# A chunked state-space scan fused with a feed-forward layer: operands at one SBUF offset, weight sums made once, another spread of the second-layer groups, later loads

## The chip, the core and the metric

The kernel runs on one core of a Trainium2 chip. Its engines are TensorE (PE in the profile; its weight loads, PEld, overlap its matmuls), VectorE (DVE), ScalarE (ACT), GpSimd (POOL) and SyncE (SP), which issues all DMAs here. The metric is the device time of the whole program in microseconds, the median of three runs.

## What is computed

The reference, cut to what matters (4 batches, 8 heads, 768 steps, head size 32, state size 16; 3072 tokens, model width 256, hidden width 2048; float32 data):

```python
# per chunk of the sequence, with state carried from chunk to chunk
cum = np.cumsum(log_a_chunk, axis=-1)
L = np.exp(cum[..., :, None] - cum[..., None, :]) * causal
M = np.einsum('bhin,bhjn->bhij', Cc, Bc) * L
y = np.einsum('bhij,bhjd->bhid', M, xc) \
    + np.einsum('bhin,bhnd->bhid', Cc, state) * np.exp(cum)[..., None]
state = np.exp(sum_log_a) * state + sum_j(Bc * xc * np.exp(cum[-1] - cum))
# y, reordered to tokens x (heads*head size) = 3072 x 256, goes through
h = y @ w_in                      # 256 -> 2048; the weights come as float64
g = np.maximum(0.01 * h, h)
return (g @ w_out).astype(np.float32)
```

## The kernel before

**Numbers.** Every float32 product is made of three TensorE matmuls on rounded halves: weight high by data high, weight low by data high, weight high by data low (`wh`, `wl`; `xh`, `xl`; `gh`, `gl`). A "product" of a 128x128 weight block with a 128x512 tile is so three matmuls of 512 columns, called large matmuls below. The weights arrive as the bits of float64 numbers (`raw`, 16 blocks `f` of 512 KB); DVE turns each into a float32 tile by five passes (abs L365, hold L372, shift L378, sign L385, low L392), ACT rounds it to `wh` (L404), POOL subtracts to `wl` (L405). `PASSES` says how many passes stand in each step.

**Startup.** Decay sums and masks are made, partly by a round trip through DRAM (`parts` to `left_d` and `right_d`, back as `dl` and `dr`), and the first three chunks of 48 steps are scanned (`LEAD`). `fetch_w` loads a weight block, `fetch_c` a chunk's B and C (`bcn`), `fetch_x` its inputs (`xs`); all are issued by SP in the order of the code, and an issue that must wait for a buffer holds what comes behind it. `keep_warm` issues matmuls on the zero tile `idle`.

**Plain phase.** 32 steps, each for one of the first two token tiles (512 tokens) and one weight block: `ffn_in` (L434, six large matmuls), `ffn_out` three steps later (L458, six). Every second step also carries the work of one of the chunks 3 to 15 (scores L283, chunk products L308 and L316, states L334 and L341, decay L250), and all carry decoding passes.

**Last phase.** `two_tiles` works on two pairs of token tiles, eight blocks `p` for each pair. In a block a pair of weight blocks meets a pair of tiles by seven products instead of eight (L627): A(a11), B(s2), C(s1), A(a12), B(s3), B(a22), C(s4). The `s` are sums of weight blocks (`weight_sums`, POOL, L575 and L584; split into halves by ACT L589 and POOL L590), made in the block before and again for the second pair. The data operands are sums of tiles, made by `combine` (L601 to L618): for the first pair at the end of the plain phase, for the second in the first pair's blocks. A is a PSUM tile of its own; B and C are the two halves of one PSUM tile, and a product that writes one of them waits until DVE has read what it must of the tile: after s2 and s1 `u2` (L696), after s3 `u3` and `c22` (L703, L704), after a22 and s4 `c21` and `c12` (L710, L711). ACT and DVE then make `gh` and `gl` (L663, L664; L667). Four second-layer groups of a block (`two_out`, L652, six large matmuls each) go into `queue`, and `slot()` issues the next one at fixed places of the block: one after C(s1), one after B(s3), two at the end. The queue starts with the last three `ffn_out` of the plain phase. A block has 21 + 24 = 45 large matmuls.

**Order.** The instructions of an engine stand in the order of the code. Tiles have places in SBUF given by pools; the byte offset that matters for the change is a tile's address modulo 2048: 1152 for `wh`, `wl`, `gh`, `gl` and the plain tiles, 2016 for the weight sums and the tiles of pool `qr`.

## Time and profile before

| | |
|---|---|
| median of 3 runs | 353.19 us (351.37 to 353.98) |
| profiled execution | 353.4 us, its span 351.7 us |
| granted TensorE clock, mean | 0.961 of full speed |
| busy: PE, DVE, ACT, POOL | 321.2, 239.7, 179.7, 176.2 us |
| large matmuls of the last phase | 738 from 161.16 us on |

A span is the time from the first to the last instruction that the profiler recorded; the profiled execution's own time is 1.7 us longer. All terms of the prediction are set against 353.4 us.

### The profile page before, as it was taken

To read this page: it belongs to the slowest core of one execution; us is meant where nothing else is said; L and a number is where in the kernel's file an instruction comes from. 1 tells how busy PE (TensorE), PEld (TensorE's weight loads), DVE (VectorE), ACT (ScalarE), POOL (GpSimd) and SP (SyncE) were. 2 spreads that over 40 slices of the span, in tenths; PEclk is the share of its full clock that TensorE was granted. 3 is DMA by queue.
4 is the path that set the end of the run, shared out by engine and by line. 5 is a ranking of instruction groups with operands and counts; after the bars stand their busy time and mean duration, and the time that the engine had idled before them with its cause. 6 is when DMAs were issued, how large, how long until landed. Compare 5 with 4: busy or idle time off the path is not lost.

```text
span 351.7 us, 8830 instructions
## 1 busy us (share of the span) xinstructions
PE 321.2 (91%) x3670; PEld 245.7 (70%) x3670; DVE 239.7 (68%) x359; ACT 179.7 (51%) x336; POOL 176.2 (50%) x259
## 2 busy tenths in 40 slices
PE   8737779989999998999887989999999999999994
PEld 3425657767777776888665767777776877778773
DVE  5839798999992232597868867877557575566651
ACT  4324555656666553443633554556545565455551
POOL 5406654766867335190627654675334653446100
PEclk9955889999999999999989999999999999999999
DMA  6564345363442200100010000000003000000003
GB/s 224 104 241 157 106 179 191 130 239 123 141 134 67 69 3 4 62 0 0 0 60 2 0 0 2 1 0 3 0 0 119 2 0 0 0 2 1 1 2 119
DMA packets 12224, 21.83 MB, mean 62 GB/s; under 512 B 4804, under 2 KB 5016, under 8 KB 12184
## 3 DMA queue, kind: packets, MB, share of 16 engines
q1 hardware_dynamic: 12184, 21.27, 18.3%
q8 instruction: 29, 0.48, 0.5%
q14 instruction: 11, 0.09, 0.1%
HBM read 17.82 MB, written 3.44 MB: 60 GB/s over the span
## 4 chain that ended last, share of the span: by engine, by line
PE 71%; DVE 16%; DMA 4%; issue 4%; ACT 3%; SPq 1%; POOL 0%; DVEq 0%; ACTq 0%
PE sc L627 17%; PE op L458 12%; PE sc L652 11%; PE hp L434 10%; PE op L652 7%; PE hp L627 5%; DVE u L703 3%; DVE c L704 3%; PE sc L283 2%; PE sc L316 2%; PE sc L308 2%; DMA bcn<-c_l 1%; DVE gl L667 1%; DMA left_d<-parts 1%; DMA xs<-x_l 1%
## 5 line engine op out<-in xcount | busy, mean ns | idle before, releaser
L590 POOL TENSOR_TENSOR sl<-s,sh 128x512 fp32r<-128x512 f32 x16 | 20.8, 1297 | 89.4 <-ACT sh L589 89.4
L341 POOL COPY xs<-stage 16x128 f32<-16x128 f32 x108 | 37.2, 345 | 40.5 <-ACT stage L334 35.3
L667 DVE TENSOR_TENSOR gl<-c,gh 128x512 fp32r<-128x512 f32 x48 | 48.8, 1020 | 8.8 <-PE op L652 5.9
L663 ACT ACTIVATE gh<-c 128x512 fp32r<-128x512 f32 x48 | 30.4, 633 | 43.0 <-DVE c L704 20.8
L441 ACT ACTIVATE gh<-hp 128x512 fp32r<-128x512 f32 x32 | 19.1, 598 | 41.3 <-PE hp L434 38.3
L447 DVE TENSOR_TENSOR gl<-hp,gh 128x512 fp32r<-128x512 f32 x32 | 21.9, 684 | 16.9 <-ACT hp L444 16.8
L627 PE MATMUL sc<-xh,sh 128*128 128x512 f32 x64 | 26.1, 408 | 5.6 <-DVE u L696 5.5
L664 ACT ACTIVATE c<-c 128x512 f32<-128x512 f32 x48 | 30.4, 633 | 1.5
L663 ACT ACTIVATE gh<-hp 128x512 fp32r<-128x512 f32 x16 | 9.6, 599 | 41.5 <-PE hp L627 41.5
L703 DVE TENSOR_TENSOR u<-sc,kept 128x512 f32<-128x512 f32 x16 | 11.1, 692 | 27.2 <-PE sc L627 27.2
L458 PE MATMUL op<-gh,wh 128*128 128x512 f32 x64 | 28.2, 440 | 0.6 <-DVE ob L472 0.6
L292 DVE TENSOR_TENSOR lt<-sc,lt 128x384 f32<-128x384 f32 x32 | 16.3, 550 | 17.3 <-PE sc L283 17.1
L575 POOL TENSOR_TENSOR w<-wh,wl 128x512 f32<-128x512 f32 x16 | 27.5, 1717 | 0.1
L434 PE MATMUL hp<-xh,wh 128*128 128x512 f32 x64 | 26.3, 411 | 1.2 <-ACT lt L259 0.9
L405 POOL TENSOR_TENSOR wl<-w,wh 128x512 fp32r<-128x512 f32 x16 | 22.2, 1390 | 9.0 <-ACT wh L404 8.1
L652 PE MATMUL sc<-gh,wh 128*128 128x512 f32 x64 | 25.3, 396 | 1.2 <-ACT ob L638 0.7
L434 PE MATMUL hp<-xh,wl 128*128 128x512 f32 x64 | 25.9, 405 | 0.0
L458 PE MATMUL op<-gl,wh 128*128 128x512 f32 x64 | 25.6, 400 | 0.0
L458 PE MATMUL op<-gh,wl 128*128 128x512 f32 x64 | 25.6, 400 | 0.0
L652 PE MATMUL op<-gh,wh 128*128 128x512 f32 x64 | 25.5, 399 | 0.0
L434 PE MATMUL hp<-xl,wh 128*128 128x512 f32 x64 | 25.5, 398 | 0.0
L652 PE MATMUL op<-gh,wl 128*128 128x512 f32 x64 | 25.4, 397 | 0.0
(140 smaller groups left out, 825.3 us busy)
## 6 DMA issues: line engine op xcount, KB each, us to landing
raw<-w_l SPq DMA_DIRECT2D x16, 512.0 KB, 3.4
bcn<-c_l SPq DMA_DIRECT2D x16, 360.0 KB, 3.9
xs<-x_l SPq DMA_DIRECT2D x32, 96.0 KB, 4.3
out_l<-ob SPq DMA_DIRECT2D x12, 256.0 KB, 2.0
dr<-right_d SPq DMA_DIRECT2D x14, 9.0 KB
right_d<-parts SPq DMA_DIRECT2D x2, 72.0 KB, 4.3
left_d<-parts SPq DMA_DIRECT2D x2, 72.0 KB
la<-a_l SPq DMA_DIRECT2D x1, 128.0 KB
```

What stands on the lines that cost most here:

```text
L341: copy(xss[c + 1][g * R:g * R + N, :, h], stage[h * D:h * D + N, g])
L405: nc.gpsimd.tensor_tensor(out=wl[:, f], in0=w32s[f], in1=wh[:, f], op=ALU.subtract)
L434: nc.tensor.matmul(hp, lhsT=w_half[h][:, f, k * 128:(k + 1) * 128], rhs=x[t][:, k, :], start=(n == 0), stop=(n == 5),)
L447: nc.vector.tensor_tensor(out=gls[s], in0=hps.pop(s), in1=ghs[s], op=ALU.subtract)
L458: nc.tensor.matmul(op, lhsT=w_half[h][:, f, DM + m * 128:DM + (m + 1) * 128], rhs=x, start=(start and i == 0), stop=(last and i == 2),)
L575: nc.gpsimd.tensor_tensor(out=w32, in0=wh[:, 2 * p:2 * p + 2, :DM], in1=wl[:, 2 * p:2 * p + 2, :DM], op=ALU.add,)
L627: nc.tensor.matmul(bank, lhsT=w[h], rhs=x[g], start=start and i == 0, stop=i == 2, skip_group_check=True,)
L652: nc.tensor.matmul(outs[t][m], lhsT=w_half[h][:, f, DM + m * 128:DM + (m + 1) * 128], rhs=x, start=start and i == 0, stop=last and i == 2,)
L663: nc.scalar.activation(gh, h, AF.Prelu, alpha=0.01)
L664: nc.scalar.activation(in_place, h, AF.Prelu, alpha=0.01)
L667: nc.vector.tensor_tensor(out=gl, in0=g, in1=gh, op=ALU.subtract)
L703: nc.vector.tensor_tensor(out=u3, in0=B, in1=kept, op=ALU.add)
```

## The change

- **Places in SBUF.** `idle` is made 944 columns wide, of which 512 are used, so that all tiles behind it lie at offset 2016 too. The data tiles get fixed places (`quad(i)`), `pob` has two buffers, `raw` three. Pools that only the startup needs (`pe`, `pcs`) are closed behind it.
- **Sums of weight blocks.** Made once for both pairs, by DVE alone with ACT's rounding: the first five at plain steps 20 to 28, the last three in blocks of the first pair. POOL has nothing to do in the last phase.
- **`combine`.** Roundings on ACT, subtractions on DVE, in four stages: for the first pair in the last four plain steps, for the second in blocks 4 to 7 of the first pair.
- **Slots.** One after C(s1), two after B(s3), one at the end. `c22`, `c21`, `c12` are written over `u3`, `kept` and `u2`.
- **Decoding.** The abs pass is ACT's (`ahead`), one block ahead; DVE has four passes, and a step four, three or two of them.
- **Loads.** A raw block is fetched when the block two before it has been decoded, not four; one instead of two is fetched beside the decay tiles at the start. The chunks from 3 on bring C already spread (912 columns, not 720), and ACT's two spreading copies go. The DRAM round trip is made in two halves. `fetch_c` and `fetch_x` of chunks 3 to 5 are issued in another order.
- **Startup.** Four filling matmuls instead of six at the start, two before the sums, two before each `decay_stack` (`WARM2`). The two later `fill_less` copies on ACT stand behind `spread_c(1)`.

```diff
-WARM = 6
-RAWS = 4
+WARM = 4
+WARM2 = 2
+RAWS = 3
...
-COMBINE = 27
-
-PASSES = (5,) * 3 + (4,) * 16
+SUMS = 20
+SUMS_AT = (20, 22, 24, 26, 27)
+
+PASSES = (4, 4, 4) + (3, 2) * 10
...
-        eng.dma_start(ins[c], c_l[c])
+        ins[c] = pin.tile([128, FAR], F32, name="bcn")
+        if c < SPREAD:
+            eng.dma_start(ins[c][:, :NEAR], c_l[c])
+        else:
+            eng.dma_start(ins[c], d_l[c - SPREAD])
...
-    idle = const.tile([128, 512], BF16, name="idle")
-    nc.vector.memset(idle, 0.0)
+                xss[c][g * R + N:(g + 1) * R].rearrange("p h b d -> p (h b d)"), x_l[c, g]
+            )
+
+    idle = const.tile([128, 944], BF16, name="idle")
+    nc.vector.memset(idle[:, :TS], 0.0)
...
+        if c >= SPREAD:
+            spread[c] = ins[c][:, C_AT:].rearrange("p (b e i) -> p b e i", b=NB, e=2)
+            return
...
+    taken = [0]
+
     def decode_abs(f):
-        w32 = w32s[f] = wst.tile([128, 2 * DM], F32, name="w32")
-        nc.vector.tensor_scalar(
-            out=w32.bitcast(U32), in0=raws[f][..., 1], scalar1=0x7FFFFFFF, scalar2=None,
-            op0=ALU.bitwise_and,
-        )
+        w32s[f] = wst.tile([128, 2 * DM], F32, name="w32")
+        nc.scalar.activation(w32s[f], raws[f][..., 1].bitcast(F32), AF.Abs)
+
+    def ahead():
+        f = len(w32s)
+        if f < NF and f in raws and f <= taken[0]:
+            decode_abs(f)
...
-        if f + RAWS < NF:
-            fetch_w(f + RAWS)
+        if f + 2 < NF:
+            fetch_w(f + 2)
...
+        second = banks()
+        keep_warm(second[:, 1], WARM2)
+        for p in range(2):
+            fill_reach(0, slice(8 * p, 8 * p + 8))
...
-        save_sums()
-        load_left(DIRECT, NC)
-        for c in range(DIRECT, DIRECT + SLOTS):
-            load_right(c)
-        fetch_w(1)
-        fetch_w(2)
...
+        save_sums(0)
+        fetch_w(1)
+        load_left(DIRECT, NC // 2)
+        for c in range(DIRECT, DIRECT + SLOTS):
+            load_right(c)
+        save_sums(1)
+        load_left(NC // 2, NC)
...
+        for b in range(2, SLOTS):
+            fill_less(b, nc.scalar.copy)
...
+                keep_warm(space[:, 0], WARM2)
...
-            decode(5)
-            if c == 0:
-                fetch_c(3)
-                fetch_x(3)
-            if c == 1:
-                fetch_w(3)
-                fetch_c(4)
-                fetch_x(4)
+            decode(4)
+            if c < LEAD - 1:
+                fetch_c(c + 3)
+            if c > 0:
+                fetch_x(c + 2)
...
-        w32 = sp.tile([128, 2, DM], F32, name="w2")
-        nc.gpsimd.tensor_tensor(
+        w32 = st.tile([128, 2, DM], F32, name="w2")
+        nc.vector.tensor_tensor(
             out=w32, in0=wh[:, 2 * p:2 * p + 2, :DM], in1=wl[:, 2 * p:2 * p + 2, :DM], op=ALU.add,
         )
         w11, w12, w21, w22 = (w32[:, i, k * 128:(k + 1) * 128] for i in range(2) for k in range(2))
-        s32 = sp.tile([128, 4, 128], F32, name="s32")
+        s32 = st.tile([128, 4, 128], F32, name="s32")
         for i, (x, y, op) in enumerate((
             (w21, w22, ALU.add), (s32[:, 0], w11, ALU.subtract), (w11, w21, ALU.subtract),
             (w12, s32[:, 1], ALU.subtract),
         )):
-            nc.gpsimd.tensor_tensor(out=s32[:, i], in0=x, in1=y, op=op)
-        wsum[p] = [s32] + [sp.tile([128, 4, 128], F32R, name=n) for n in ("sh", "sl")]
-
-    def sums_split(p):
-        s32, sh, sl = wsum[p]
+            nc.vector.tensor_tensor(out=s32[:, i], in0=x, in1=y, op=op)
+        yield
+        wsum[p] = sh, sl = [sp.tile([128, 4, 128], F32R, name=n) for n in ("sh", "sl")]
         nc.scalar.copy(sh, s32)
-        nc.gpsimd.tensor_tensor(out=sl, in0=s32, in1=sh, op=ALU.subtract)
+        nc.vector.tensor_tensor(out=sl, in0=s32, in1=sh, op=ALU.subtract)
...
+        ah, t12, th12, t34 = new(F32R, "ah"), new(F32, "t12"), new(F32R, "th12"), new(F32, "t34")
+        nc.scalar.copy(ah, a)
+        sub(t12[:, 0], b[:, 0], a[:, 0])
+        sub(t12[:, 1], b[:, 1], t12[:, 0])
+        sub(t34[:, 0], b[:, 1], b[:, 0])
...
-            if q is not None:
-                weight_sums(q)
+            go((p, 0))
             slot()
             product(A, False, a12, x["21"])
             act_split(A, g["11"][0], A)
             product(B, False, s3, x["t3"])
             nc.vector.tensor_tensor(out=u3, in0=B, in1=kept, op=ALU.add)
-            nc.vector.tensor_tensor(out=c22, in0=C, in1=u3, op=ALU.add)
+            nc.vector.tensor_tensor(out=u3, in0=C, in1=u3, op=ALU.add)
             low(g["11"][1], A, g["11"][0])
-            act_split(c22, g["22"][0], c22)
+            act_split(u3, g["22"][0], u3)
+            go((p, 1))
+            slot()
             slot()
             product(B, False, a22, x["t4"])
             product(C, False, s4, x["22"])
-            nc.vector.tensor_tensor(out=c21, in0=B, in1=kept, op=ALU.add)
-            nc.vector.tensor_tensor(out=c12, in0=C, in1=u2, op=ALU.add)
-            low(g["22"][1], c22, g["22"][0])
-            if q is not None:
-                sums_split(q)
-            act_split(c21, g["21"][0], c21)
-            low(g["21"][1], c21, g["21"][0])
-            act_split(c12, g["12"][0], c12)
-            low(g["12"][1], c12, g["12"][0])
-            next(beside, None)
+            nc.vector.tensor_tensor(out=kept, in0=B, in1=kept, op=ALU.add)
+            nc.vector.tensor_tensor(out=u2, in0=C, in1=u2, op=ALU.add)
+            low(g["22"][1], u3, g["22"][0])
+            act_split(kept, g["21"][0], kept)
+            low(g["21"][1], kept, g["21"][0])
+            act_split(u2, g["12"][0], u2)
+            low(g["12"][1], u2, g["12"][0])
             slot()
-            slot()
-            order = ("11", "22", "21", "12") if q is not None else ("11", "21", "22", "12")
+            order = ("11", "22", "21", "12")
+            if p == NP - 1 and pair == PAIRS[-1]:
+                order = ("11", "21", "22", "12")
...
+        if s == SUMS:
+            settle()
+            assert len(ready) == NF
+            wts.close()
+            st = ctx.enter_context(
+                tc.tile_pool(name="st", bufs=1, side="right", reuse_waits="tile")
+            )
+            sp = ctx.enter_context(
+                tc.tile_pool(name="sp", bufs=NP, side="right", reuse_waits="tile")
+            )
         if s == OUT[NC - 1] + 1:
-            settle()
             scan.close()
-            qr = ends.enter_context(
-                tc.tile_pool(name="qr", bufs=12, side="right", reuse_waits="tile")
-            )
-            sp = ends.enter_context(
-                tc.tile_pool(name="sp", bufs=2, side="right", reuse_waits="tile")
-            )
-            su = ends.enter_context(
-                tc.tile_pool(name="su", bufs=1, side="right", reuse_waits="tile")
-            )
-            weight_sums(0)
-            sums_split(0)
-            combining = combine(PAIRS[0], [qr] * 10)
-        next(combining, None)
+            qr = ctx.enter_context(tc.tile_pool(name="qr", bufs=1, reuse_waits="tile"))
+            su = ctx.enter_context(tc.tile_pool(name="su", bufs=2, reuse_waits="tile"))
+            combining = combine(PAIRS[0], (0, 1, 8, 9, 10, 11, 4, 12, 5))
...
+        if s - 1 in SUMS_AT:
+            next(summing, None)
+        if s in SUMS_AT:
+            summing = weight_sums(SUMS_AT.index(s))
+            next(summing)
+        if s >= total - 4:
+            next(combining, None)
+    next(combining, None)
     queue.extend([lambda s=s: ffn_out(s) for s in range(total - LAG, total)])
     cross = banks()
-    for i, pair in enumerate(PAIRS):
-        more = i + 1 < len(PAIRS)
-        beside = combine(PAIRS[i + 1], [qr] * 4 + [quads] * 6) if more else iter(())
-        two_tiles(pair, cross[:, 0], cross[:, 1], more, beside)
+    beside = {}
+    both = combine(PAIRS[1], (2, 3, 1, 9, 13, 14, 6, 3, 7))
+    for i in range(4):
+        beside[i + 4, 1] = [both]
+    for i, p in enumerate(range(len(SUMS_AT), NP), 1):
+        work = weight_sums(p)
+        beside[i, 1] = beside[i + 1, 0] = [work]
+    for pair in PAIRS:
+        two_tiles(pair, cross[:, 0], cross[:, 1], beside if pair == PAIRS[0] else {})
...
```

On TensorE, in a block of the last phase, from the second matmul of B(s3) on, before (`sc` is the tile of B and C, `op` a second-layer output):

```order
L627 MATMUL sc<-xh,sl 128x512
L627 MATMUL sc<-xl,sh 128x512
L652 MATMUL op<-gh,wh 128x512
L652 MATMUL op<-gh,wl 128x512
L652 MATMUL op<-gl,wh 128x512
L652 MATMUL op<-gh,wh 128x512
L652 MATMUL op<-gh,wl 128x512
L652 MATMUL op<-gl,wh 128x512
L627 MATMUL sc<-xh,wh 128x512
L627 MATMUL sc<-xh,wl 128x512
```

and after, from the last matmul of B(s3) to that of a second group; the first of a22, `sc<-th_3212,wh`, comes behind it:

```order
L650 MATMUL sc<-tl_3373,sh 128x512
L675 MATMUL op<-gh,wh 128x512
L675 MATMUL op<-gh,wl 128x512
L675 MATMUL op<-gl,wh 128x512
L675 MATMUL op<-gh,wh 128x512
L675 MATMUL op<-gh,wl 128x512
L675 MATMUL op<-gl,wh 128x512
L675 MATMUL sc<-gh,wh 128x512
L675 MATMUL sc<-gh,wl 128x512
L675 MATMUL sc<-gl,wh 128x512
L675 MATMUL sc<-gh,wh 128x512
L675 MATMUL sc<-gh,wl 128x512
```

The second group (here one whose output lies in a tile that is named `sc` too) has moved from the end of the block to the place before a22.

On DVE, in a block of the first pair, before:

```order
L696 TENSOR_TENSOR u_3027<-sc,kept 128x512
L703 TENSOR_TENSOR u_3028<-sc,kept 128x512
L704 TENSOR_TENSOR c_3029<-sc,u_3028 128x512
L667 TENSOR_TENSOR gl<-hp,gh 128x512
L710 TENSOR_TENSOR c_3030<-sc,kept 128x512
L711 TENSOR_TENSOR c_3031<-sc,u_3027 128x512
L667 TENSOR_TENSOR gl<-c_3029,gh 128x512
L667 TENSOR_TENSOR gl<-c_3030,gh 128x512
L667 TENSOR_TENSOR gl<-c_3031,gh 128x512
L614 CAST xh<-t_2809 128x1024
```

and after, in one that carries a stage of `combine`:

```order
L720 TENSOR_TENSOR u_3179<-sc,kept 128x512
L726 TENSOR_TENSOR u_3180<-sc,kept 128x512
L727 TENSOR_TENSOR u_3180<-sc,u_3180 128x512
L690 TENSOR_TENSOR gl<-hp,gh 128x512
L620 TENSOR_TENSOR t_3132<-x_1873,t_3130 128x512
L620 TENSOR_TENSOR al<-x_1873,ah 128x1024
L735 TENSOR_TENSOR kept<-sc,kept 128x512
L736 TENSOR_TENSOR u_3179<-sc,u_3179 128x512
L690 TENSOR_TENSOR gl<-u_3180,gh 128x512
```

The stage of `combine`, which stood behind the block's three `gl`, now stands in front of the two reads after s4 (L735, L736).

On SP, from the first store of the decay sums on, before:

```order
L206 DMA right_d<-parts 128x6x48
L210 DMA left_d<-parts 128x2x144
L206 DMA right_d<-parts 128x6x48
L210 DMA left_d<-parts 128x2x144
L217 DMA dl<-left_d 48x14x48 x2
L223 DMA dr<-right_d 6x768 x4
L86 DMA raw<-w_l 128x1024 x2
L223 DMA dr<-right_d 6x768
L86 DMA raw<-w_l 128x1024
L90 DMA bcn<-c_l 128x720
L99 DMA xs<-x_l 48x512 x2
```

and after:

```order
L214 DMA left_d<-parts 128x2x144
L218 DMA right_d<-parts 128x6x48
L92 DMA raw<-w_l 128x1024
L225 DMA dl<-left_d 48x6x48 x2
L231 DMA dr<-right_d 6x768 x4
L214 DMA left_d<-parts 128x2x144
L218 DMA right_d<-parts 128x6x48
L225 DMA dl<-left_d 48x8x48 x2
L231 DMA dr<-right_d 6x768
L92 DMA raw<-w_l 128x1024
L99 DMA bcn<-d_l 128x912
```

One raw block has moved ahead of the decay tiles' loads, the other behind them, and the second half of the sums is stored behind the loads of the first.

## Rows read from the trace of the kernel before

**Rows 1.** The page: TensorE's line of its first part (busy microseconds, share of the span, instructions), the queue by which the engines' programs come, of its third (packets, megabytes, share of 16 engines), and the shares of the chain that ended last by engine, of its fourth.
```profile
PE 321.2 (91%) x3670; PEld 245.7 (70%) x3670; DVE 239.7 (68%) x359; ACT 179.7 (51%) x336; POOL 176.2 (50%) x259
...
q8 instruction: 29, 0.48, 0.5%
...
PE 71%; DVE 16%; DMA 4%; issue 4%; ACT 3%; SPq 1%; POOL 0%; DVEq 0%; ACTq 0%
```

**Rows 2.** The table by windows, of the startup and the plain phase: the window, its length, the busy time of each engine (instructions), TensorE's granted clock as a part of full speed, the share of the DMA engines, GB/s.
```profile
20.00:25.00 5.00, 0.26 (x17) 0.07 (x5) 0.61 (x1) 0.00 (x0) 0.00 (x0) 0.50 0.69 250
...
30.00:35.00 5.00, 4.10 (x83) 2.83 (x67) 4.81 (x13) 2.22 (x5) 2.94 (x5) 0.50 0.63 219
...
40.00:45.00 5.00, 2.87 (x33) 1.76 (x22) 4.86 (x10) 2.39 (x6) 4.48 (x9) 1.00 0.27 94
...
90.00:120.00 30.00, 30.00 (x734) 23.89 (x733) 19.30 (x32) 19.65 (x42) 19.09 (x38) 1.00 0.31 93
120.00:161.00 41.00, 39.36 (x534) 31.69 (x533) 21.20 (x27) 18.28 (x37) 20.08 (x35) 1.00 0.06 19
```

**Rows 3.** The chain of waits up to 62 us: start, length, what the chain consisted of.
```profile
20.26 4.86 issue
...
32.24 4.55 DMA bcn<-c_l
```

**Rows 4.** SP's queue: the wait of the raw weight loads (total us, times, longest), and the loads themselves in the page's last part (KB each, median us from issue to landing).
```profile
SPq L86 <- DVE w L392: 36.0, 10, 4.9
...
raw<-w_l SPq DMA_DIRECT2D x16, 512.0 KB, 3.4
```

**Rows 5.** The table by windows, one row for a block `p` of the last phase (from the first `hp<-xh,wh` of L627 to the next block's): four blocks of the first pair of tiles, one of the second.
```profile
161.16:170.60 9.44, 9.32 (x41) 7.25 (x39) 5.73 (x9) 3.91 (x7) 0.97 (x1) 1.00 0.00 0
170.60:185.18 14.58, 12.16 (x47) 9.47 (x45) 10.85 (x16) 6.58 (x13) 7.38 (x8) 0.88 0.10 37
185.18:198.32 13.14, 10.91 (x46) 8.29 (x45) 10.48 (x12) 5.86 (x11) 8.66 (x8) 1.00 0.00 0
...
221.58:232.44 10.86, 10.73 (x46) 8.29 (x45) 8.10 (x11) 5.87 (x11) 6.40 (x7) 1.00 0.00 1
...
287.24:298.02 10.78, 10.66 (x46) 8.36 (x45) 6.82 (x10) 5.87 (x11) 5.42 (x7) 1.00 0.00 0
```

**Rows 6.** What the weight loads of TensorE waited for in the last phase (total us, times, longest): in the first pair, 161.16 to 254.11, and then in the second, 254.11 to the end.
```profile
PEld sc L627 <- DVE u L696: 7.8, 6, 2.9
PEld sc L627 <- DVE c L704: 3.9, 7, 0.6
...
PEld sc L627 <- DVE c L704: 4.4, 8, 0.6
PEld sc L652 <- ACT ob L638: 1.1, 1, 1.1
PEld sc L652 <- DVE ob L640: 0.9, 1, 0.9
```

**Rows 7.** The timeline around one wait (start, length, engine, line, operation, tiles, and in brackets the idle time before it and what ended it).
```profile
270.30 0.39 PE L627 MATMUL sc<-xl,sh 128*128 128x512 f32 x1
...
270.73 0.69 DVE L703 TENSOR_TENSOR u<-sc,kept 128x512 f32<-128x512 f32 x1 [1.94 <-PE sc L627]
...
271.46 0.69 DVE L704 TENSOR_TENSOR c<-sc,u 128x512 f32<-128x512 f32 x1
...
271.69 0.39 PE L652 MATMUL op<-gl,wh 128*128 128x512 f32 x1
...
272.20 0.19 PEld L627 LDWEIGHTS sc<-xh,wh 128*128 128x128 f32 x1 [0.55 <-DVE c L704]
...
272.54 0.40 PE L627 MATMUL sc<-xh,wl 128*128 128x512 f32 x1
...
273.46 0.39 PE L627 MATMUL sc<-xl,sh 128*128 128x512 f32 x1
...
274.50 0.68 DVE L711 TENSOR_TENSOR c<-sc,u 128x512 f32<-128x512 f32 x1
```

**Rows 8.** TensorE's timeline: in the plain phase the first and the last of the six L434 matmuls of a step and the first of the step two later; then, in the last phase, the first and the last of 27 matmuls in a row.
```profile
98.99 0.39 PE L434 MATMUL hp<-xh,wh 128*128 128x512 f32 x1
...
100.12 0.39 PE L434 MATMUL hp<-xl,wh 128*128 128x512 f32 x1
...
107.10 0.39 PE L434 MATMUL hp<-xh,wh 128*128 128x512 f32 x1
...
287.24 0.40 PE L627 MATMUL hp<-xh,wh 128*128 128x512 f32 x1
...
293.27 0.39 PE L652 MATMUL op<-gl,wh 128*128 128x512 f32 x1
```

**Rows 9.** Durations. L667, the subtraction on DVE with both inputs in SBUF (tile `c`; ns min/median/max, first and last start): in 337 to 352 us, where POOL is idle, and in 260 to 337, where it works; then groups of instructions by line over the whole span (busy us, mean ns; idle time before, and what ended it).
```profile
L667 DVE TENSOR_TENSOR gl<-c,gh x3: 682/692/693, 339.8 to 342.5; 128x512 fp32r<-128x512 f32 x3
...
L667 DVE TENSOR_TENSOR gl<-c,gh x21: 692/869/1297, 263.5 to 331.7; 128x512 fp32r<-128x512 f32 x21
...
L575 POOL TENSOR_TENSOR w<-wh,wl 128x512 f32<-128x512 f32 x16 | 27.5, 1717 | 0.1
...
L365 DVE TENSOR_SCALAR w<-raw 128x512 uint32<-128x512 uint32 x16 | 11.0, 689 | 0.0
...
L341 DVE COPY xs<-stage 16x128 f32<-16x128 f32 x12 | 3.2, 268 | 5.8 <-ACT stage L334 5.4
```

More of the change, by code (lines that the diff above doesn't have):

```diff
@@ L55, in scan_ffn @@
 @with_exitstack
[L56 removed]
+def scan_ffn(ctx: ExitStack, tc: tile.TileContext, a_l, c_l, d_l, x_l, w_l, out_l):
     nc = tc.nc
@@ L112, in scan_ffn @@
     keep_warm(first[:, 1], WARM)
-    la = pc.tile([128, NC * NM], F32, name="la")
+    la = pe.tile([128, NC * NM], F32, name="la")
     nc.sync.dma_start(la, a_l)
@@ L133, in scan_ffn @@
     dr = pc.tile([128, SLOTS, NM, Q], BF16, name="dr")
-    reach = [pc.tile([128, NM, Q], F32, name=f"reach{i}") for i in range(DIRECT)]
+    reach = [pe.tile([128, NM, Q], F32, name=f"reach{i}") for i in range(DIRECT)]
     nc.vector.memset(upto, 1.0)
@@ L406, in settle @@
             ready.add(f)
+        ahead()
     def do_low(f):
@@ L511, in scan_ffn @@
             fill_less(b, nc.gpsimd.tensor_copy)
-        for b in range(2, SLOTS):
-            fill_less(b, nc.scalar.copy)
+        for g in range(2):
+            nc.gpsimd.memset(xss[0][g * R:g * R + N], 0.0)
         decay_exp(0, pds[0], True)
+        for g in range(2):
+            nc.tensor.matmul(
+                second[g * R:(g + 1) * R, 0, :NC * NM], lhsT=half(after, g), rhs=half(la, g),
+                start=True, stop=True,
+            )
+        nc.scalar.activation(erev, second[:, 0, :NC * NM], AF.Exp)
+        save_sums(0)
[5 more added lines that the diff above has]
+        load_left(NC // 2, NC)
         sc = banks()
         scores(0, sc)
-        for g in range(2):
-            nc.tensor.matmul(
-                first[g * R:(g + 1) * R, 1, :NC * NM], lhsT=half(after, g), rhs=half(la, g),
-                start=True, stop=True,
-            )
-        nc.scalar.activation(erev, first[:, 1, :NC * NM], AF.Exp)
-        nc.vector.tensor_copy(
-            dl[:Q].rearrange("p c g r -> p c (g r)"),
-            ub[:Q].rearrange("p g r -> p (g r)").unsqueeze(1).to_broadcast([Q, NC, 2 * R]),
-        )
         weigh(0, sc)
+        state_decay(0)
         decay_direct(1, pds[1])
@@ L592, in scan_ffn, with combine @@
     rhs = {}
[L594 to L601 removed]
+    def combine(pair, places):
+        a, b = (x32[t] for t in pair)
+        place = iter(places)
+        new = lambda dtype, n: quad(next(place), dtype, n)
+        sub = lambda out, x, y: nc.vector.tensor_tensor(
+            out=out, in0=x, in1=y, op=ALU.subtract
+        )
+        ah, t12, th12, t34 = new(F32R, "ah"), new(F32, "t12"), new(F32R, "th12"), new(F32, "t34")
[3 more added lines that the diff above has]
+        sub(t34[:, 0], b[:, 1], b[:, 0])
@@ L673, in slot, with two_tiles, go @@
             queue.popleft()()
-    def two_tiles(pair, B, C, more, beside):
+    def two_tiles(pair, B, C, beside):
+        def go(name):
+            for work in beside.get(name, ()):
+                next(work, None)
         t1, t2 = pair
```

171 lines of the change are left out of this document (81 added, 90 removed).

## The prediction

> **What bounds the kernel now.** I read the page first. TensorE is busy for 91% of the span and holds 71% of the chain that ended last, DVE 16% and "issue" 4% [rows 1], so time can be won only where TensorE is not fed or not at pace. The tables by window say where that is. In the plain phase it never is: from 90 to 120 us it is busy for 30.00 of 30 [rows 2]. Two stretches are left. In the startup it is busy for 0.26 of the five microseconds from 20 and for 2.87 of those from 40, where DVE is busy for 4.86 [rows 2]. In the last phase one block of 45 large matmuls takes 10.78 us in the second pair of tiles, and 14.58, 13.14 and 10.86 in three blocks of the first [rows 5]. The waits of the last phase [rows 6] name who is late: DVE each time, twice through an output copy.
>
> **What the last phase loses.** The usual wait stands in the timeline [rows 7]. After product B(s3) DVE makes `u` (L703, 270.73) and `c` (L704, ends at 272.15); a22 writes the same PSUM tile and starts at 272.20. The matmul before started at 271.69, and in step the next would have come at 271.92, so 0.28 us are lost, and 0.11 more at the next one (272.20 to 272.54 where 0.23 is usual): 0.39 per wait, 0.16 less than the 0.55 that the weight load's row shows. There are 7 + 8 such waits [rows 6], 5.9 us. The six waits for `u` L696 in the first pair cost 7.8 − 6 × 0.16 = 6.8. Behind the longest the granted clock of the block is 0.88 [rows 5]: 14.58 × 0.12 / 0.5 = 3.5 us at 1.2 GHz, half of them lost, 1.7. The output copy L640 costs 0.9 − 0.16 = 0.7. Sum 15.1. The wait on L638 (1.1) lies in the tail, in the last block of the last pair, and stays.
>
> **Part 1, spread of the second-layer groups.** Two groups instead of one stand between B(s3) and a22. A group is 6 matmuls, 1.38 us at 0.23 each (270.30 to 271.69, six gaps [rows 7]). DVE is done 272.15 − 270.69 = 1.46 us after the last matmul of s3 (270.30, 0.39 long) [rows 7]; the cover goes from 1.38 to 2.76. The 15 waits go: −5.9. The price is on the other side: only one group and the next block's a11 (1.38 + 0.69 = 2.07) now stand between C(s4) and the next block's B(s2), which needs both reads of the tile done. s4's last matmul ends at 273.85 and the second read, L711, at 275.18: 1.33 us if DVE is free. Margin 0.7; DVE may be late by that before TensorE waits. In the first block no group is queued yet for that slot, so a11 alone covers (0.69): a stall of 0.6 to 0.9, once.
>
> **Part 2, sums of weight blocks once, no work on POOL.** Before, POOL makes them 16 times, with L575 alone 1717 ns each [rows 9], beside DVE's own subtractions: L667 takes 692 ns in the last 15 us, where POOL has nothing to do, and 869 in the median of 260 to 337 us, up to 1297 [rows 9]. That DVE time makes `u` L696 late. After, POOL has no work in the last phase, so DVE's nine operations of a block take 9 × 0.69 = 6.2 us at most. The sums that DVE takes over cost one addition and one subtraction of 512 columns (0.69 each, as L667 undisturbed) and four of 128 columns, whose duration on DVE no row shows: between 0.27 (a copy of 16x128 [rows 9]) and 0.69; I take 0.3, nearer to the row of their width: 2.6 in all (bounds 2.5 to 4.1). Five of the eight fall in steps 20 to 28, three in the first pair's first blocks: 6.2 + 2.6 = 8.8 (10.3 at the bound) against 45 × 0.23 = 10.35 of TensorE. Operands of the second pair follow in blocks 4 to 7, three subtractions of 512 columns in the fullest, 6.2 + 2.1 = 8.3. In the block as a whole DVE has room; in order behind a sum or a combine step, it is late at C(s4) by up to 0.3 in some blocks. I put 0.4 for all of those beside 0.9 for the first block: 1.3 given back. The 6.8 + 1.7 + 0.7 go.
>
> The Trainium skill says in "SBUF — State Buffer", section "Who interferes with whom", that a DVE instruction with two SBUF inputs contends with a GpSimd instruction that reads SBUF. By that rule L667 would lose its surplus altogether; the trace agrees, with 692 ns beside 869.
>
> **Part 3, one offset for all operands.** In the plain phase six L434 matmuls, whose weights and data lie at one offset, start 226 ns apart (98.99 to 100.12, five gaps). In the last phase data and sums lie elsewhere, and 26 gaps from 287.24 to 293.27 are 232 each [rows 8]. The 738 matmuls of the phase (16 blocks of 45 and 18 of the plain phase's last steps) give (232 − 226) × 738 = 4.4 us at most, nothing at least; other products in the first pair have both operands at the second offset, and they show no better pace, so that the offset is the cause is open. I take a third, 1.5.
>
> The Trainium skill gives, in "TensorE: Matmul & The Clock Gate", section "Back-to-back issue gap", N/2.4 + 2.5 ns, 216 for 512 columns, and in the SBUF page's section named above that TensorE never waits on anyone. By these the offset would change nothing; the trace's 226 to 232 differ from 216, but not by which part.
>
> Last phase: −15.1 + 1.3 − 1.5 = −15.3.
>
> **Part 4, startup and first steps (to about 62 us).** Four things. (a) "issue" at 20.26, 4.86 us [rows 3]: TensorE waits for nothing that the profile shows, while the queues move 250 GB/s [rows 2] and TensorE's program itself comes by a queue (29 packets [rows 1]). Of the two raw loads that are issued together in that burst, the change has one ahead of it and one behind. Between 0 and −4.9; I take −3, as these are its longest loads. (b) SP stood 36.0 us in ten waits of a raw load for DVE's last pass, up to 4.9, with the scan's loads queued behind [rows 4]; one of these, bcn, is the chain for 4.55 us from 32.24 [rows 3]. Now a raw load takes a buffer that was read a block before, and SP waits no more: 0 to −4, I take −2. (c) DVE loses the abs pass, 0.69 [rows 9], once in each of three startup chunks and each weight block, and fewer passes stand in a step; DVE is full from 30 to 35 and from 40 to 45 [rows 2]: at least 6 passes of 0.69 in the stretch, −4.1 if all count; I take −3.5. (d) Against it ACT takes the abs (0.69 at most, if it is as slow there as on DVE), the later fill copies in front of the first state copies, and TensorE gets up to eight filling matmuls of 0.23 to 0.43: +1.5 (0 to 3.5). Sum −7, bounds −2 and −10. The clock is 0.50 there in rows of idle TensorE [rows 2]; I count no gain of it.
>
> **Part 5, plain phase.** DVE loses passes, ACT loses two copies per chunk, and a chunk's load grows by 27% (912 columns for 720); TensorE has no idle time to give there [rows 2]. The sums go to DVE, which is busy for 21.20 of 41 us from 120 on, while TensorE is for 39.36 [rows 2]; the 1.6 us that it lacks may shrink: −0.5 (0 to −1.5).
>
> **Sum.** Of the profiled execution's 353.4 us: −15.3 − 7 − 0.5 gives 330.6, and 331 in round numbers; the median of the runs, 353.19, is 0.2 away. Bounds of the terms together: last phase −11 to −18, startup −2 to −10, plain 0 to −1.5, which gives 324 to 340, and 325 to 336 without all ends at once.
>
> **Rivals.**
> 1. The stall moves. The two reads after s4 come late at every block's end, since only 2.07 us cover them. It decides once DVE is over 0.7 us late at C(s4); at 1.2 us late, 16 × 0.5 = 8 come back: 338. For it: DVE was late by more in the first pair. Against it: without POOL it has two idle microseconds per block.
> 2. The offset gives nothing, and mixed pace stays, or all matmuls take the slower one: 330.6 + 1.5 = 332 without a gain, 334 with 384 plain-phase matmuls 5 ns slower (+1.9). For it: products at the second offset show no better pace. It also covers that the change doesn't do what it says. By the rule of the Trainium skill named in part 3 (the page on TensorE) the first of these would come.
> 3. The startup gives nothing: "issue" stays as long, and ACT's new work fills what DVE gave up: 330.6 + 7 = 338. For it: the reason of the 4.86 is only inferred.
> 4. The clock comes up sooner, since filling matmuls bridge the startup's gaps: of the 15 us from 20 to 35 TensorE worked for some 8 at 0.50 (4.10 of the last five [rows 2]); half of that back, and the next stretch with it, gives 327 to 322.
> 5. Slower than before: weights come late. A raw load is now issued two blocks ahead, not four, and a block is decoded every 1.6 steps at 2.5 passes a step, 6.5 us by two steps of 8.11 us (98.99 to 107.10 [rows 8]). Loads landed in 3.4 us [rows 4]; with a half step, 2.0, in which the block's matmuls still come behind others, the plain phase stalls once they take over 8.5, and with 11.5 in ten blocks, 3 us each, it ends at 331 + 30 = 361. Against it: that is almost three times what they took.
>
> **How the numbers follow.** Forecast 331 with its own range 325 to 336: 0.50. Rival 1 0.15, rival 2 0.15, rival 3 0.12, rival 4 0.05, rival 5 0.03. The range 321 to 341 takes in all but rival 5 and the ends of the others. One per cent, 3.5 us, is about what a measurement of this kernel can tell from no change. Only rival 5, or rivals 1 and 3 together with no gain of the offset and a new wait, come within it or above: faster 0.95, same 0.03, slower 0.02.
>
> **What the profile after would show.** Blocks of the last phase at 10.2 to 10.5 us in both pairs, no PEld wait for the DVE sum behind B(s3), one short wait in the first block; L690 near 690 ns; gaps of 226 to 229 ns between large matmuls; the last phase starting at 153 to 154 us, not 161.16 [rows 5]; no "issue" row above 2 us in the startup. I am wrong if blocks stay above 10.7 (then which wait is new), or if the last phase starts as late as before.

## The result and the profile after

The changed kernel takes 336.44 us (336.17 to 338.87, four runs) against 352.68 of the kernel before beside it: a ratio of 0.9555, 95% interval 0.9497 to 0.9613. In a second series on the chip it took 338.13 (337.08 to 340.91, six runs) against 353.08: 0.9589, 0.9555 to 0.9622. The gain is 15 to 16 us where 22 were forecast. The forecast of 331 is missed by 5 to 7 us: inside the range of 321 to 341, but above its own of 325 to 336. The profiled execution took 336.55 us, its span 334.8. Executions more than 1.5% above the fastest of their kernel are left out of the medians and ranges below (one each of shift16, raws2, idle512, pool_busy, pool_block and abs_dve, two of nofill_raws2).

The page after: busy times, TensorE's clock in 40 slices, the chain by engine, to be read against [rows 1].

```profile
PE 311.2 (93%) x3676; PEld 245.5 (73%) x3676; DVE 224.8 (67%) x386; ACT 180.4 (54%) x326; POOL 80.1 (24%) x161
...
PEclk9957879999997999999999999999999999999998
...
PE 87%; issue 5%; DVE 3%; ACT 2%; POOL 1%; ACTq 0%; POOLq 0%
```

DVE has left the chain (16% to 3%), and "issue" has grown to 5%. The last phase by blocks, as in [rows 5]:

```profile
160.87:169.71 8.84, 8.84 (x41) 7.32 (x39) 5.84 (x9) 2.94 (x5) 0.00 (x0) 1.00 0.03 12
169.71:180.92 11.21, 10.51 (x46) 8.37 (x45) 8.60 (x16) 5.68 (x10) 0.00 (x0) 1.00 0.11 39
180.92:191.12 10.20, 10.20 (x46) 8.45 (x45) 8.04 (x16) 5.77 (x11) 0.00 (x0) 1.00 0.00 0
211.52:221.72 10.20, 10.20 (x46) 8.45 (x45) 7.59 (x12) 6.19 (x11) 0.00 (x0) 1.00 0.00 0
283.53:293.73 10.20, 10.20 (x47) 8.45 (x45) 5.85 (x10) 5.25 (x10) 0.00 (x0) 1.00 0.00 0
```

Most blocks take 10.20 us, with TensorE busy for all of it; the second (11.21), the eighth (10.70) and the tenth (10.31) are longer, and the first, which issues fewer second-layer groups, is shorter. The waits of TensorE's weight loads from 155 us to the end (as [rows 6]) and the first and the last of 27 matmuls in a row (as [rows 8]):

```profile
PEld sc L650 <- DVE u L736: 1.7, 2, 1.1
PEld sc L675 <- ACT ob L661: 1.1, 1, 1.1
PEld sc L650 <- DVE u L720: 0.2, 1, 0.2
...
283.53 0.39 PE L650 MATMUL hp<-ah,wh 128*128 128x512 f32 x1
...
289.42 0.39 PE L675 MATMUL op<-gl,wh 128*128 128x512 f32 x1
```

The wait behind B(s3) is gone; 5.89 us for 26 gaps is 226.5 ns, where it was 232. DVE's subtraction of 512 columns with both inputs in SBUF is back at its undisturbed time (lines of the two pages, before and after):

```profile
L667 DVE TENSOR_TENSOR gl<-c,gh 128x512 fp32r<-128x512 f32 x48 | 48.8, 1020 | 8.8 <-PE op L652 5.9
...
L690 DVE TENSOR_TENSOR gl<-u,gh 128x512 fp32r<-128x512 f32 x32 | 22.0, 687 | 7.9 <-ACT u L687 7.9
```

From the first large matmul to the last the phase took 186.18 us before (161.16 to 347.34) and takes 169.64 (160.87 to 330.51): −16.5.

So all of the gain stands in the last phase, and the phase starts as late as before, at 160.87 instead of 161.16. The table by windows of what comes ahead of it, as [rows 2]:

```profile
20.00:25.00 5.00, 1.50 (x58) 1.20 (x49) 1.13 (x4) 0.65 (x2) 0.21 (x1) 0.50 0.33 127
...
30.00:35.00 5.00, 3.48 (x19) 2.44 (x16) 4.82 (x12) 2.32 (x5) 2.62 (x6) 1.00 0.96 316
...
40.00:45.00 5.00, 4.25 (x16) 2.95 (x16) 3.72 (x8) 1.94 (x4) 2.77 (x6) 0.50 0.34 120
...
90.00:120.00 30.00, 28.42 (x597) 22.42 (x597) 19.94 (x31) 17.10 (x34) 18.55 (x36) 0.94 0.42 132
120.00:157.00 37.00, 35.56 (x517) 28.46 (x516) 23.28 (x51) 19.05 (x35) 8.37 (x23) 1.00 0.07 24
```

From 90 to 120 us TensorE was busy for 30.00 of 30 at full clock; it now lacks 1.6 us, and the clock is 0.94. By the first matmul of a step (L434 before, L454 after): step 6 started at 61.90 before and 58.60 after, step 15 at 98.99 and 95.34, step 16 at 104.02 and 103.56, the last phase at 161.16 and 160.87. Of 3.65 us won by step 15, 3.2 are lost in that one step. TensorE's timeline shows it:

```profile
98.06 0.38 PE L294 MATMUL sc<-bcn 32*64 32x96 f32 x4
100.03 0.88 PE L294 MATMUL sc<-bcn 32*64 32x96 f32 x28 [1.58 <-issue]
100.83 0.80 PE L478 MATMUL op<-gh,wh 128*128 128x512 f32 x1
...
103.13 0.63 PE L478 MATMUL op<-gl,wh 128*128 128x512 f32 x1
103.56 0.63 PE L454 MATMUL hp<-xh,wh 128*128 128x512 f32 x1
```

Amid the 32 score matmuls of a chunk TensorE stops for 1.58 us, and the large matmuls behind start 0.43 us apart from 101.42 to 103.98 where 0.23 is usual; the clock that was granted there is 1.2 GHz. Gaps that are released by nothing stand in the startup's chain too (as [rows 3]):

```profile
20.29 3.50 issue
...
37.43 3.32 issue
```

### The profile page after: what moved, and what is told of

Read it like the earlier page. It is cut to its first block, busy times and chain, and to the rows that moved or that the text cites. A ratio compares the mean times of both kernels' runs of the same rounds, so it can differ in the third digit from the quotient of the medians.

```text
span 334.8 us, 8694 instructions
## 1 busy us (share of the span) xinstructions
PE 311.2 (93%) x3676; PEld 245.5 (73%) x3676; DVE 224.8 (67%) x386; ACT 180.4 (54%) x326; POOL 80.1 (24%) x161
## 4 chain that ended last, share of the span: by engine, by line
PE 87%; issue 5%; DVE 3%; ACT 2%; POOL 1%; ACTq 0%; POOLq 0%
PE sc L650 16%; PE op L478 14%; PE hp L454 14%; PE sc L675 13%; PE op L675 12%; PE hp L650 6%; PE sc L294 3%; PE sc L327 2%; PE sc L319 2%; PE sc L258 1%; PE sc L117 1%; POOL xs L353 1%; POOL bcn L282 1%; ACT lt L267 0%; PE pd L250 0%
## 5 line engine op out<-in xcount | busy, mean ns | idle before, releaser
L686 ACT ACTIVATE gh<-u 128x512 fp32r<-128x512 f32 x32 | 20.0, 625 | 17.8 <-DVE u L727 17.8
L454 PE MATMUL hp<-xh,wh 128*128 128x512 f32 x64 | 26.6, 415 | 1.5 <-ACT lt L267 1.5
L690 DVE TENSOR_TENSOR gl<-u,gh 128x512 fp32r<-128x512 f32 x32 | 22.0, 687 | 7.9 <-ACT u L687 7.9
L424 POOL TENSOR_TENSOR wl<-w,wh 128x512 fp32r<-128x512 f32 x16 | 23.1, 1447 | 16.7 <-ACT wh L423 16.0
L454 PE MATMUL hp<-xh,wl 128*128 128x512 f32 x64 | 25.8, 403 | 0.0
L686 ACT ACTIVATE gh<-kept 128x512 fp32r<-128x512 f32 x16 | 10.1, 632 | 28.8 <-DVE kept L735 28.8
L454 PE MATMUL hp<-xl,wh 128*128 128x512 f32 x64 | 25.6, 400 | 0.0
L478 PE MATMUL op<-gl,wh 128*128 128x512 f32 x64 | 25.5, 399 | 0.0
L675 PE MATMUL sc<-gh,wl 128*128 128x512 f32 x64 | 24.9, 389 | 0.0
L675 PE MATMUL sc<-gl,wh 128*128 128x512 f32 x64 | 24.9, 389 | 0.0
L675 PE MATMUL op<-gl,wh 128*128 128x512 f32 x64 | 24.9, 389 | 0.0
```

Source lines behind the costliest of these rows:

```text
L424: nc.gpsimd.tensor_tensor(out=wl[:, f], in0=w32s[f], in1=wh[:, f], op=ALU.subtract)
L454: nc.tensor.matmul(hp, lhsT=w_half[h][:, f, k * 128:(k + 1) * 128], rhs=x[t][:, k, :], start=(n == 0), stop=(n == 5),)
L478: nc.tensor.matmul(op, lhsT=w_half[h][:, f, DM + m * 128:DM + (m + 1) * 128], rhs=x, start=(start and i == 0), stop=(last and i == 2),)
L675: nc.tensor.matmul(outs[t][m], lhsT=w_half[h][:, f, DM + m * 128:DM + (m + 1) * 128], rhs=x, start=start and i == 0, stop=last and i == 2,)
L686: nc.scalar.activation(gh, h, AF.Prelu, alpha=0.01)
L690: nc.vector.tensor_tensor(out=gl, in0=g, in1=gh, op=ALU.subtract)
```

## The experiments

**What the gaps are.** If TensorE waited there for its own program, which comes in packets, the gaps would end at fixed steps of its instruction count. Counting the trace's records of TensorE (weight loads, matmuls and its recorded semaphore events) up to the end of each "issue" gap of more than half a microsecond gives 450, 706, 1473, 2498, 4033 and 5569 in the kernel after: 193 or 194 modulo 256 each time. Before, the gaps at 25.12, 42.22, 49.33 and 136.58 end at 705, 1474, 1730 and 5569, 193 or 194 again. (One gap in the startup of each, at counts 486 and 484, is of another kind.) The queue that brings the programs moved 29 packets of 16 KB each, before [rows 1] and after, and the 7404 records of TensorE in the kernel after are 28.9 times 256. Before each of these gaps ends such a packet lands, 1.3 to 1.6 us before TensorE goes on: the one of 97.51 to 98.71 us ahead of 100.03.

Shifted by 16 instructions:

```diff
     keep_warm(first[:, 1], WARM)
+    for _ in range(8):
+        nc.tensor.matmul(first[:, 1, :8], lhsT=idle[:, :128], rhs=idle[:, :8], start=True, stop=True)
```

> The changed kernel with eight matmuls of 8 columns more at its very start (16 more TensorE instructions, about 0.3 us beside the first loads), nothing else. In the changed kernel three plain-phase gaps of the kind 'issue' (at 65.34, 100.03 and 136.20 us) and those of the startup end at instructions whose number on TensorE is 193 or 194 modulo 256, and 256 instructions of 64 bytes are one packet of 16 KB on the queue that brings the program. Theory 1, TensorE waits there for its next 256 instructions: with 16 more ahead the boundaries fall 16 instructions earlier in the chunk work, the gaps of 1.58 and 1.44 us at 100 and 136 go with the half clock behind the first (about 1.7 us): 336.4 - 4.7 + 0.3 = 332. Theory 2, the gaps belong to the chunk's own data or semaphores at these places: they stay, 336.4 to 336.7.

It took 334.95 us in the middle of its runs (334.04 to 338.70; the profile is of the last). The timelines of TensorE, of the shifted kernel and (last row) of the kernel after:

```profile
85.47 0.31 PE L329 MATMUL sc<-lt,xs 64*32 64x48 f32 x12 [1.34 <-issue]
...
103.77 0.27 PE L329 MATMUL sc<-lt,xs 64*32 64x48 f32 x3 [1.79 <-issue]
...
137.99 0.89 PE L296 MATMUL sc<-bcn 32*64 32x96 f32 x32
```

```profile
136.20 0.48 PE L294 MATMUL sc<-bcn 32*64 32x96 f32 x10 [1.44 <-issue]
```

The gap in the scores at 136 us is gone (32 matmuls in one piece, and 55.2 us from step 16 to the last phase where it was 57.3). The one at 100 has moved some 16 instructions back in the program, from the scores into the chunk products (L329 here), and ends at a count of 4031, 191 modulo 256; the gaps from 41 us on in this trace all end at 190 or 191, the two before at 193 or 194 (a few records are missing in each trace). The short one at 65.34 is gone too, and new ones came at 61.45 and 85.47. So theory 1 holds for what the gaps are, and its forecast of 332 does not: moving the boundaries took gaps away and made others.

**The startup's loads.** Two raw buffers:

```diff
-RAWS = 3
+RAWS = 2
```

> The changed kernel with two raw buffers, so that the load of raw block 2, and the chunk load queued behind it on SP, are issued once block 0 is decoded (about 28 us) and not at 17.4 us. Theory 1a, the program's packet stands behind these loads (968 KB from 17.4 on; the packet began at 21.42 and the gap of TensorE lasted from 20.29 to 23.79): the gap shrinks to about 1.8 us, the plain phase starts 1.7 us earlier: 334.7, if the later loads don't come late in their turn. Theory 1b, the packet is late for another reason: the gap stays 3.5 us, 336.4 or more, since SP now waits at each raw block.

It took 335.78 us (334.10 to 337.12); the profile is of an execution of 341.22. Its chain of waits and, of SP's waits, the raw blocks' (as [rows 4]), then those of the kernel after:

```profile
22.84 1.86 issue
...
32.45 5.02 DMA xs<-x_l
...
39.71 2.38 issue
```

```profile
SPq L92 <- DVE w L411: 54.4, 14, 7.8
```

```profile
SPq L92 <- DVE w L411: 8.2, 4, 3.3
```

The gap shrank as 1a said, 3.50 to 1.86 us. In the other profiles it is 2.04 to 3.78 with three buffers and 2.32 with two (nofill_raws2), so the number of buffers alone does not set it. What it goes with is the loads ahead of the packet. From the start of the chunk products in front of the gap to the start of the packet 1.08 us pass in raws2, where no other load begins in between; 2.63 in the kernel after, where loads of 0.82 MB do; 4.17 before, with 1.45 MB. The time of the kernel is 0.7 us below the changed kernel's first median, within the spread: SP waits 54.4 us in all where it waited 8.2 after and 36.0 before [rows 4], and a load that is late behind it, 5.02 us at 32.45, now stands in the chain.

**The spread of the groups.** Undone in the kernel after (one, one, two), and made alone in the kernel before:

```diff
             go((p, 1))
             slot()
-            slot()
...
             slot()
+            slot()
```

> The changed kernel with the old spread of the second-layer groups (one after C(s1), one after B(s3), two at the end), all else as changed. The prediction's part 1: the wait for the sum behind B(s3) is back in each of 16 blocks at 0.39 us: 336.4 + 6.2 - 1.0 (the two waits at B(s2) that the change brought) = 341.6. The rival, that the old waits came from DVE being slowed by POOL: no wait, 336.4.

> The kernel before with the new spread of the second-layer groups alone (one after C(s1), two after B(s3), one at the end). The prediction's part 1 by itself: the 15 waits behind B(s3) go, 5.9 us; DVE, which POOL still slows, is later at the block's end, where one group less covers it: 352.8 - 5.9 = 347 with nothing given back, 349 with 0.3 us more in the first pair's blocks. The rival 'the stall moves': the waits before B(s2) take over, 352 or more.

Undone: 342.51 us; the wait is back in every block, a block takes 10.66, and the last phase takes 176.94, 7.3 more:

```profile
PEld sc L650 <- DVE u L727: 9.2, 16, 0.6
```

Alone in the kernel before: 350.15, only 2.7 less. The waits of its first pair, and a block of each pair:

```profile
PEld sc L627 <- DVE u L696: 10.1, 6, 3.3
```

```profile
182.79:197.85 15.06, 12.18 (x46) 9.49 (x45) 10.33 (x12) 5.75 (x11) 9.04 (x8) 0.89 0.00 1
286.39:296.78 10.39, 10.39 (x46) 8.45 (x45) 6.68 (x10) 5.76 (x11) 5.43 (x7) 1.00 0.00 0
```

In the second pair the 0.39 us per block came; in the first the stall moved to B(s2), 10.1 us where 7.8 stood [rows 6]. That is rival 1, in the place and for the reason that the prediction gave it, but only while DVE is slow.

**GpSimd beside DVE.** Four additions of 128x512 on GpSimd per block, into a tile that nobody reads, free to run ahead, and then with the first one tied to the block:

```diff
             go((p, 0))
+            junk = st.tile([128, 2, DM], F32, name="junk")
+            for k in range(4):
+                nc.gpsimd.tensor_tensor(
+                    out=junk, in0=wh[:, 2 * p:2 * p + 2, :DM], in1=wl[:, 2 * p:2 * p + 2, :DM],
+                    op=ALU.add if k else ALU.subtract,
+                )
```

> The changed kernel with four additions of 128x512 on GpSimd in each block of the last phase, into a tile that nobody reads (about 7 us of GpSimd per block, as the sums took before): the price of GpSimd's work beside DVE's. Theory (prediction, part 2): DVE's subtraction with two SBUF inputs goes from 0.69 to 0.87 us and more, DVE is late before B(s2) in the first pair, where it also has sums and combine steps: 3 to 6 us, 339 to 342. Rival: with two groups behind B(s3) and fewer DVE operations there is room enough, 336.4 to 337.

> The changed kernel with four additions of 128x512 on GpSimd in each block, into a tile that nobody reads, the first of them on the block's own tile kept, so that GpSimd works some 5.5 us in each block of 10.2, as it did before, and doesn't run ahead as in pool_busy. Theory: in the first pair DVE has 6.2 + 2.6 us of work undisturbed and some 2.4 more beside GpSimd, 11.2 against 10.2: about 1 us late in each of seven blocks, and none in the second pair: 340 to 344. Rival: pool_busy cost 30 us because GpSimd worked without a pause, and half the load fits into DVE's free time: 336.4 to 338.

The free one took 366.13 us. A stretch of its first pair shows DVE and GpSimd both full and TensorE starved:

```profile
200.00:220.00 20.00, 16.36 (x57) 12.87 (x58) 19.18 (x22) 9.16 (x16) 18.98 (x14) 0.83 0.00 0
```

The tied one took 337.44, inside the range of its rival (336.4 to 338), and its last phase 171.10, 1.5 us more than 169.64. The waits that grew stand in the first pair, 3.8 us where the kernel after has 1.7. These waits and the durations of DVE's small sums, first of this kernel, then of the kernel after:

```profile
PEld sc L650 <- DVE u L744: 3.8, 7, 1.2
...
L608 DVE TENSOR_TENSOR s<-w 128x128 f32<-128x128 f32 x6 | 4.6, 774 | 0.1
```

```profile
L608 DVE TENSOR_TENSOR s<-w 128x128 f32<-128x128 f32 x6 | 1.7, 288 | 0.1
```

DVE does slow down beside GpSimd (288 to 774 ns), but only what falls together, and in 10.2 us there was room for most of it. The subtractions L690, which were slowed most before, keep their 687 ns here, so that this run doesn't bring the old collision back. How much of the first pair's old stalls was GpSimd's doing, and how much the roundings of `combine` that also left DVE, no run separates.

**The offset.** The idle tile narrow again:

```diff
-    idle = const.tile([128, 944], BF16, name="idle")
+    idle = const.tile([128, 512], BF16, name="idle")
```

> The changed kernel with the idle tile 512 columns wide as before, so that every tile behind it lies 864 bytes lower, and only those of the right side keep offset 2016. If the common offset is what brought the pace of the last phase from 232 to 226.7 ns: gaps between large matmuls back at 229 to 232 ns, 738 x 2.5 to 5 ns = 1.8 to 3.9 us: 338 to 340. If not: 226.7 ns stay, 336.4.

It took 339.48 us. A block of the second pair, again without any idle time of TensorE:

```profile
284.59:294.92 10.33, 10.33 (x46) 8.45 (x45) 5.86 (x10) 5.25 (x10) 0.00 (x0) 1.00 0.00 0
```

10.33 / 45 is 229.6 ns where 226.7 stood: the last phase takes 171.38 us, 1.7 more, with the same instructions. The places of operands in SBUF do set TensorE's pace, if by nanoseconds; that a common offset is what matters of them is not shown.

**The startup's other parts.** The filling matmuls of before (warm_old), none but those at the start (nofill), the same with two raw buffers (nofill_raws2), the changed kernel once more (after_again), and the abs pass on DVE:

```diff
-WARM = 4
-WARM2 = 2
+WARM = 6
+WARM2 = 0
```

> The changed kernel with the filling matmuls of before (six at the start, none before the sums and the decay stacks): 12 TensorE instructions fewer, so that the 256-instruction boundaries lie 12 later in the program. If the gap at 100 us is set by where the boundary falls in the chunk work, it goes, as in the kernel before, where it was not: 336.4 - 3.3 = 333, or 335 if the filling matmuls saved 2 us in the startup. If it is set by the moment (the loads and waits around that chunk), it stays there at the boundary's new place, 1.5 us and 1.7 of half clock: 336.4 to 338.

> The changed kernel without the filling matmuls before the sums and the decay stacks (eight of 512 columns, at 1.2 GHz 0.43 us each where the clock is half). Theory, the filling matmuls lie on the path of the startup (the chain shows two of them, 0.88 us from 4.57, and the run with the old filling was 2.2 us shorter): 333 to 334.5. Rival, that run was short by chance or by where the program's boundaries fell: 336 to 337.

> As nofill, and two raw buffers, so that 968 KB of loads leave the burst behind which the program's packet stood (with three fillings the gap at that boundary was 2.1 us with two buffers, 2.7 to 3.6 with three). If that packet's wait is on the path: 1 us below nofill. If the time until the first step is set elsewhere, or SP's waits give it back: the same as nofill, or above.

> The changed kernel unaltered, beside the others on the same chip, since runs of it differ by up to 2.7 us: 336.4, between 335.5 and 337.5.

```diff
-        nc.scalar.activation(w32s[f], raws[f][..., 1].bitcast(F32), AF.Abs)
+        nc.vector.tensor_scalar(
+            out=w32s[f].bitcast(U32), in0=raws[f][..., 1], scalar1=0x7FFFFFFF, scalar2=None,
+            op0=ALU.bitwise_and,
+        )
```

> The changed kernel with the abs pass on DVE again (16 passes of 0.69 us, at the places where ACT has them now). The prediction's term c counts 2 to 3.5 us in the startup for the pass that DVE lost: 338.5 to 340. If the startup hangs on TensorE's program and the loads instead, DVE's pass is hidden: 336.4 to 337.

| kernel | median us (range) | step 6 at | step 15 to 16 | last phase at |
|---|---|---|---|---|
| before | 352.7 to 353.1 | 61.90 | 5.03 | 161.16 |
| after | 336.44 (336.17 to 338.87) | 58.60 | 8.22 | 160.87 |
| after, once more | 338.13 (337.08 to 340.91) | 61.39 | 7.96 | 162.79 |
| warm_old | 334.15 (332.38 to 336.63) | 55.50 | 6.17 | 156.73 |
| nofill | 336.38 (335.02 to 338.66) | 58.29 | 8.28 | 160.51 |
| nofill_raws2 | 335.44 (334.80 to 335.80) | 56.14 | 5.04 | 159.70 |
| abs_dve | 338.19 (334.13 to 338.28) | 59.37 | 6.86 | 158.47 |

The last three columns are of one profiled execution each. After, once more, nofill and nofill_raws2 ran in one series, in five rounds: without the filling matmuls the kernel is 1.75 us faster by the medians, with ranges that overlap. The changed kernel itself, at 338.13, came out 0.6 above what was expected of it, and its two profiles differ by 3 us at step 6. The gap in step 15 stands in five of these six profiles of changed kernels, with 1.1 us lost in warm_old (whose boundary lies 12 instructions later) and without half a clock there, and not in nofill_raws2. Which chunk meets the gap is so not set by the boundary's place alone. What differs is when the packet begins. In the three profiles without a gap in this chunk (before, before_slots, nofill_raws2) it begins 1.9 to 2.3 us before TensorE starts the instruction at the boundary ahead of it; in the eleven with one, 0.1 to 1.2 us after. The abs pass on DVE costs nothing that these runs can tell. warm_old is 2.3 us below the changed kernel's first median and nofill 1.75 below its second; their intervals against the kernel before, 0.938 to 0.9536 and 0.9502 to 0.9567, overlap with the changed kernel's, so that neither is shown to beat it. Only nofill_raws2 lies clear of it, 0.9477 to 0.9530 against 0.9555 to 0.9622 in the same series, and two of its six executions, left out here, took 340.7.

## Why the prediction was right in range and too low

**Last phase: −15.3 forecast, −16.5 measured.** Part 1's wait goes as told; undoing the spread costs 7.3 us in the phase, 0.46 a block where 0.39 was read: the wait and the late start behind it are 0.42, and the other starts are a nanosecond further apart. Part 2's waits for `u` go; against the 1.3 us given back, 1.5 are lost (the rows show 1.7 + 0.2), most of it in the second block (11.21 us), since the first block's last slot is empty, as foreseen. Part 3 was mis-sized: 1.5 was taken of 4.4. The stretches by which a start came later than 227 ns after the one before, by more than a few nanoseconds, sum to 15.1 us before and 1.5 after (without the tail's wait), so that of 16.5 us the pace gave 2.9; 1.7 of it goes with the idle tile's width alone, the rest with no single edit that was run.

The Trainium skill's rule that TensorE never waits on anyone ("SBUF — State Buffer", "Who interferes with whom") would have left the pace as it was; idle512 differs from the changed kernel in nothing but addresses and runs at 229.6 ns, so here the measurement decides against reading it that far.

**Startup: −7 forecast, −3.3 and −0.5 measured by step 6 in two executions.** This is the term that failed, and the prediction's own sign of it came: the last phase starts as late as before. (a) The prediction costed one of five "issue" gaps of TensorE. Up to 62 us they sum to 10.5 us before and 9.8 after, not to 3 less: the gap at 20.29 shrank from 4.86 to 3.50, but another of 3.32 stands at 37.43. That most of them are waits for TensorE's program was argued in the prediction and is now shown by their counts (the gap at counts 484 and 486 is not one of them); that loads ahead of the packet lengthen one of them holds (4.17, 2.63 and 1.08 us above), but that moving two loads would shorten the sum was wrong. (b) SP's waits did go (36.0 to 8.2 us), and no row of this execution's chain in the startup names a load; what that won is not separated. (c) The freed DVE pass was worth nothing measurable: abs_dve takes 338.19 us and has step 6 at 59.37. From 40 to 45 us DVE is now busy for 3.72 where it was for 4.86 [rows 2], beside a TensorE that waits for its own program until 40.75. (d) The filling matmuls cost about 1.75 us by the medians, not clear of the spread, near the 1.5 that was put for them and ACT's work.

**Plain phase: −0.5 forecast; from step 6 to the last phase +3.0 and +2.1 measured.** Up to step 15 it won 0.35 us in the profiled execution and 1.5 in the other one (step 6 to 15: 37.09 before, 36.74 and 35.55), then lost 3.2 and 2.9 in step 15. "No idle time to give" [rows 2] was right, and the error was to take a full stretch as safe: a chunk's 160 small matmuls are 320 instructions, and run in 2.1 us; if 256 of them lie between two boundaries, a packet that begins only at the first comes too late for the second. Why it began earlier for the same chunk before (at 98.57 for use at 101.86) and not after (97.51 for 100.03) is open. The 1.6 us that TensorE lacked from 120 to 161 us, of which the prediction hoped for 0.5, were such a gap too (1.64 at 136.58) and stayed (1.44 at 136.20).

So the total is inside the range because the last phase came out as costed and a little better, and because the range took rival 3 in. That rival came true in its size, 160.87 against 161.16, for a mixture of its reason and this new gap; its 338 and the better last phase make 336.4. Rival 1 is real, but only in the kernel before, with its slower DVE. Rival 2 is refuted. Rival 4 came in part: from 30 to 35 us the granted clock is 1.00 where it was 0.50 [rows 2], but from 40 to 45 it is 0.50 where it was 1.00. Rival 5 did not come: no wait of TensorE for `wl` stands in the plain phase.

## What to carry to other kernels

Before a stall in front of TensorE is put down to data, count its instructions up to it: if the counts of several stalls agree modulo 256, TensorE waits there for its program, and a freed vector pass will not move them; loads of data move one only where they keep its packet waiting. Two edits that relieve the same engine should be costed together: in the last phase the new spread gave 2.7 us alone and 7.3 on top of a relieved DVE. And what was won in a phase whose engine is full came out the same each time (169.62 to 169.66 us in the profiles of all seven kernels that keep it), while time saved in this startup, which hangs on several queues, was lost again at the next one.

## What the runs showed of the hardware

- TensorE stops at some of its boundaries of 256 instructions, for 0.6 to 4.9 us in the kernels before and after, where it gets there before the packet has landed or just behind it; in the two kernels' gaps the packet of 16 KB took 0.9 to 1.9 us, and TensorE went on 1.3 to 1.6 us after it had landed. At 96.82 and 132.88 in the kernel after, boundaries amid small matmuls (6.5 ns an instruction), the packet began 0.7 and 0.9 us behind, and the next boundary cost 1.58 and 1.44 us. The Trainium skill ("Runtime: NRT & Kernel Launch", "Instruction fetch mechanics") has the blocks of 256 instructions and calls the cost of a boundary mostly hidden; the first the trace agrees with, the second in the last phase, where the packets landed 29 us and more ahead, but not at these boundaries.
- Behind a gap of 1.58 us amid work the granted clock fell to 1.2 GHz in the changed kernel; behind one of 1.45 in abs_dve (in the same step) it did not: its clock is 1.00 from 90 to 120 us. The length of the gap does not decide it, since behind 1.81 us in pool_block, in the same step, it did not fall either.
- The same matmuls on the same data run 226.7 ns apart (the kernel after) or 229.6 (idle512) by the addresses of their operands alone.
